# Sums of quarters one step earlier, and transfers given out in the opening

## The chip, the cores and the metric

The kernel runs on one core of a Trainium2 chip. The metric is the time of one execution in microseconds (us); the median of three runs is used, and 0.3% is about what a measurement of this kernel can tell from no change.

## The reference

Attention within chunks of 64 tokens, and behind it a gated feed-forward layer over all 4608 tokens, in float32:

```
q, k, v: (8, 8, 576, 64)              # batch, heads, tokens, width; 9 chunks of 64
scores = q_c @ k_c.T / 8              # within a chunk
attn   = softmax(scores)
x      = (attn @ v_c) laid out as (4608, 512)
g      = x @ w_gate                   # (512, 1536)
silu   = g / (1 + exp(-g))
val    = x @ w_val                    # (512, 1536)
out    = (silu * val) @ w_out         # (1536, 512)
```

## The kernel before

The tokens are cut into nine batches of 512 columns, and the inner width of 1536 into twelve pieces of 128. Handling one piece is a *step*, counted here from f = 0, so that the sixth step is step 5. A float32 number is held as two float32r parts, hi and lo, and a product of two such numbers is three matmuls (lo by hi, hi by lo, hi by hi), since `x` and the weights are split so everywhere.

The first two batches (`a0`, `a1`) go through the twelve steps together, while the weights come in for the first time. The weights arrive as raw 64-bit words; ScalarE (ACT) and VectorE (DVE) make float32 of them (`scale`, `shift`, `below`, `join`), split them (`upper` on ACT, `lower` on DVE), and what is made is stored to DRAM for the later batches (`save_w` the weights of gate and value, `save_o` those of the output).

A plain step does four products of 12 matmuls on TensorE (PE): gate and value of batch 0, gate and value of batch 1, and between them the projection of the step before (12 matmuls): 60 matmuls. In the steps from `SEVEN` on (`first_seven`) the four products of the two batches are made by Strassen's scheme instead: seven products of 6 matmuls, of sums of quarters of the weights with sums of quarters of x, 54 matmuls with the projection. For these are needed:

- four sums of the quarters of x, S1, S2, S4 and S5 (`Raw`, made by DVE: `whole` adds the hi and lo of a part of x, `both` combines two), and their hi and lo (`upper` on ACT, `lower` on DVE). Their places are the tiles w8 and w9; the split ones lie in w0 to w3, where the weights of steps 0 to 3 had been, once these are stored.
- in each step the sums of quarters of the next step's weights (`Quarters`: `sums` on DVE into `ts`, `upper` on ACT, `lower` on DVE). Their place, `th`, has one buffer in the steps up to `SEVEN`, and `save` stores it in two halves (`t<-th` in the profile). From `SEVEN` on every second step uses the place of batch 1's first x instead (`odd_t`).

The order of the work on PE, ACT and DVE is the order of the code, and in these first steps that of the transfers on the SyncE queue (SP) as well: each engine takes its instructions in that order, and one that waits holds up all behind it. In steps 1 to `SEVEN` - 1, `ahead`, `beside` and `within` are tables by step: what stands in them is put in before the gate's product, behind the shifts of the raw words, and behind the multiplication of batch 0's gate by its value. That multiplication (`times`, L519) reads the value's PSUM bank and so frees it for PE; there are two such banks (`ps_gv`) for the four products in turn.

Before step 1 stands an opening with a written order of its own (`opening`), in which the scores and columns of the two batches and step 0 are computed. Its loads are issued on SP in the first 15 us.

The later batches are computed from the stored weights; the change doesn't touch them.

Of the kernel before, what the change touches and what calls it, by code (L numbers as in the profile page):

```python
# [8 lines left out]
F32 = mybir.dt.float32  # L9
# [5 lines left out]
ALU = mybir.AluOpType  # L15
AX = mybir.AxisListType

P = 128
# [4 lines left out]
NK = DM // P  # L23
# [10 lines left out]
def attn_then_gated_ffn(ctx: ExitStack, tc: tile.TileContext, qk, v, wgv, wo, out):  # L34
# [102 lines left out]
    class Quarters:  # L137
# [12 lines left out]
            engine.tensor_tensor(out=s[:, 3], in0=t[:, 1], in1=s[:, 2], op=ALU.subtract)  # L150

        def place(self):
            if self.f >= SEVEN and self.f % 2:
                if not odd_t:
                    odd_t.extend(xs.tile([P, 4 * Q], F32R, name="th", tag=tag) for tag in ("xh0", "xl0"))
                return list(odd_t)
            both = const.tile([P, 2, 4 * Q], F32R, name="th", tag="th")
            return [both[:, 0], both[:, 1]]
# [11 lines left out]
                nc.sync.dma_start(out=kept_t[self.f][:, j], in_=self.halves[j].bitcast(F32))  # L170

    odd_t = []
    SEVEN, EARLY = 6, 4

    def moved(i):
        return f"w{(i + EARLY) % NF}"
# [18 lines left out]
    def save_w(f):  # L195
        kept_w[f] = store.tile([P, 2, 4 * Q], F32, name=f"w{f}")
        nc.sync.dma_start(out=kept_w[f], in_=w_both[f].bitcast(F32))
# [290 lines left out]
    def save_o(f):  # L488
        nc.sync.dma_start(out=kept_o[f], in_=out_now[f].bitcast(F32))
# [229 lines left out]
    for do in opening.split():  # L719
        if do[0] == ".":  # L720
            keep_warm(int(do[1:]))
        elif do[0] in "gvw":
            getattr(weights[do[:-1]], steps[do[-1]])()
        elif do[0] in "GV":
            if do[0] not in products:
                products[do[0]] = Product(a0, 0, "GV".index(do[0]))
            products[do[0]].add((int(do[3]), int(do[4])))
        elif do[0] == "e":
            a0.exchange(v0[int(do[1])][:, 1], values[int(do[1])][1], nc.scalar.copy)
        elif do == "H0":  # L730
            h0 = silu(products["G"].ps)
        elif do == "Q0":
            times(h0, products["V"].ps)
        else:
            b, i = int(do[1]), int(do[2])
            pairs = do[0] in "STCUL"
            getattr(couples[b, i // 2 if pairs else i], do[0])(i if pairs else int(do[3:] or 0))
    w = up[1]
    pg, pv = Product(a1, 0, 0), Product(a1, 0, 1)
    pg.add((0, 1), (1, 1), (0, 2), (1, 2), (2, 1), (3, 1), (2, 2), (3, 2))  # L740
# [5 lines left out]
    pv.add((0, 0), (1, 0), (2, 1), (3, 1), (2, 2), (3, 2), (2, 0), (3, 0))  # L746
    pv1 = pv.ps
    w.lower()
    o.shift()
    o.join()  # L750
    quarters = Quarters(1)
# [1 line left out]
    p0 = parts(a0, 0, h0)  # L753
    wo_f = out_weights(0)
    lag(p0, wo_f)
    down[1].load()
    down[1].scale()
    quarters.upper()

# [1 line left out]
    class Raw:  # L761


        def __init__(self):
            self.at = [const.tile([P, 2, NK // 2 * N], F32, name="sums", tag=tag) for tag in ("w8", "w9")]
            self.split = {}

        def place(self, i):
            return self.at[i[0]][:, i[1]]

        def whole(self, a, c, to):
# [22 lines left out]
    def begin():  # L794
        raw.append(Raw())
        raw[0].whole(a1, 0, S4)
        raw[0].whole(a1, 1, S1)

    ahead = {3: lambda: raw[0].upper(1, 0), 4: lambda: raw[0].upper(2, 1)}
    beside = {2: begin,  # L800
              3: lambda: (raw[0].whole(a0, 0, S2), raw[0].both(S4, S2, S4, ALU.subtract)),
              4: lambda: (raw[0].lower(2), raw[0].upper(4, 2)),
              5: lambda: (raw[0].whole(a0, 1, S5), raw[0].both(S5, S5, S2, ALU.subtract), raw[0].upper(5, 3))}
    within = {2: lambda: raw[0].both(S1, S1, S4, ALU.add),
              3: lambda: (raw[0].lower(1), raw[0].both(S2, S1, S2, ALU.subtract)),
              4: lambda: raw[0].lower(4), 5: lambda: raw[0].lower(5)}

    for f in range(1, SEVEN):
        w, o = up[f + 1], down[f]
        save_o(f - 1)  # L810
        up[f + 2].load()
        if f <= EARLY:
            save_w(f - 1)
        if f > 2:
            quarters.save()
        down[f + 1].load()
        ahead.get(f, lambda: None)()
        h0 = gate(a0, f)
        times(h1, pv1)
        put_off(h1)  # L820
        if f <= 2:
            quarters.lower()
            quarters.save()
        quarters = Quarters(f + 1)
        w.shift()
        w.below()
        pv0 = value(a0, f)
        o.shift()
        o.below()
        beside.get(f, lambda: None)()  # L830
        w.join()
        w.upper()
        times(h0, pv0)
        within.get(f, lambda: None)()
        p0 = parts(a0, f, h0)
        w.lower()
        o.join()
        quarters.sums(w.t)
        up[f + 2].scale()
        wo_f = out_weights(f)  # L840
        lag(p0, wo_f)
        h1 = gate(a1, f)
        quarters.upper()
        down[f + 1].scale()
        if f > 1:
            quarters.lower()
        pv1 = value(a1, f)
# [15 lines left out]
    def turns(which):  # L863

        if pending:
            project(*pending[0], which=which)
            if T - 1 in which:
                pending.pop()

    def first_seven(f, done, before):  # L870
# [29 lines left out]
        if w:  # L900
            w.join()
            w.upper()
        nc.scalar.copy(out=v2, in_=ps2)
        turns([0])
        product(ps1, 2, False)
        quarters = Quarters(f + 1)
        if w:
            quarters.sums(w.t)
            w.lower()
        nc.scalar.copy(out=v1, in_=ps1)  # L910
        if w:
            quarters.upper()
# [406 lines left out]
```

## Time and profile before

| | |
|---|---|
| runs, us | 902.27, 904.18, 905.06; median 904.18 |
| the profiled execution | 903.28, of which the span from first to last instruction is 901.5 |
| PE busy in the span | 885.2 (98%) |
| granted TensorE clock | 1.000 |
| mean of DMA moved | 248 GB/s |
| sizes of one transfer | weights stored `w<-w`, raw weights `raw<-in_wgv`, raw output weights `raw<-in_wo`: 1024 KB; `o<-both` and each half of `t<-th`: 512 KB; `h<-h`: 256 KB |
| silu of 128x512 on ACT | 599 ns (mean of L1153) |

A row of a timeline gives the start, the length, the engine (SPq and ACTq are the issues of transfers on SP and ACT), the line, the operation with output and input, and in brackets how long the engine stood idle ahead of it and what it waited for. A row of stretches gives the busy time of each engine between two moments, the granted clock, the share of time that the DMA engines were busy, and GB/s.

### The profile page before, as it was taken

To read this page: it belongs to the slowest core of one execution; us is meant where nothing else is said; L and a number is where in the kernel's file an instruction comes from. 1 tells how busy PE (TensorE), PEld (TensorE's weight loads), DVE (VectorE), ACT (ScalarE), POOL (GpSimd) and SP (SyncE) were. 2 spreads that over 40 slices of the span, in tenths; PEclk is the share of its full clock that TensorE was granted. 3 is DMA by queue.
4 is the path that set the end of the run, shared out by engine and by line. 5 is a ranking of instruction groups with operands and counts; after the bars stand their busy time and mean duration, and the time that the engine had idled before them with its cause. 6 is when DMAs were issued, how large, how long until landed. Compare 5 with 4: busy or idle time off the path is not lost.

```text
span 901.5 us, 14751 instructions
## 1 busy us (share of the span) xinstructions
PE 885.2 (98%) x6047; PEld 731.7 (81%) x6047; DVE 545.6 (61%) x834; ACT 386.1 (43%) x587; POOL 17.1 (2%) x18
## 2 busy tenths in 40 slices
PE   7998999999999999999999999999999999999998
PEld 6776788878888888888888888888888888888886
DVE  5869899853787655775763646776645533333332
ACT  4846677653514335324233445234334432223232
POOL 1200000000021000000000000000000000000000
PEclk9999999999999999999999999999999999999999
DMA  9297977799898657755586857665667565556651
GB/s 358 112 377 264 323 291 274 291 315 349 271 359 286 253 198 258 258 213 180 217 294 236 333 185 282 233 228 195 220 245 242 212 237 201 196 220 233 234 187 47
DMA packets 73170, 223.25 MB, mean 248 GB/s; under 512 B 30736, under 2 KB 30992, under 8 KB 58896
## 3 DMA queue, kind: packets, MB, share of 16 engines
q1 hardware_dynamic: 71664, 219.70, 67.3%
q10 hardware_dynamic: 1440, 2.62, 0.8%
q8 instruction: 47, 0.77, 0.3%
q14 instruction: 19, 0.16, 0.0%
HBM read 178.78 MB, written 43.52 MB: 247 GB/s over the span
## 4 chain that ended last, share of the span: by engine, by line
PE 90%; DMA 4%; DVE 4%; ACT 1%; issue 1%; POOL 0%; SPq 0%; ACTq 0%
PE ps_a L857 25%; PE ps_gv L857 19%; PE ps_o L538 11%; PE ps_o L539 10%; PE ps_o L540 10%; PE ps_gv L475 10%; DMA t<-th 3%; PE ps_a L287 2%; PE ps_a L365 1%; DMA qk_t<-in_qk 1%; ACT th L162 0%; DVE sums L776 0%; PE ps_a L451 0%; PE ps_a L465 0%; DVE th L165 0%
## 5 line engine op out<-in xcount | busy, mean ns | idle before, releaser
L857 PE MATMUL ps_a<-x,factors 128*128 128x512 f32 x864 | 219.3, 389 | 0.0
L857 PEld LDWEIGHTS ps_a<-x,factors 128*128 128x128 f32 x864 | 162.2, 188 | 33.7
L857 PE MATMUL ps_gv<-x,factors 128*128 128x512 f32 x648 | 164.5, 389 | 0.0
L857 PEld LDWEIGHTS ps_gv<-x,factors 128*128 128x128 f32 x648 | 121.7, 188 | 25.2
L538 PE MATMUL ps_o<-both,hl 128*128 128x512 f32 x336 | 132.3, 394 | 0.2 <-DVE hl L63 0.2
L539 PE MATMUL ps_o<-both,hh 128*128 128x512 f32 x336 | 131.0, 390 | 0.0
L540 PE MATMUL ps_o<-both,hh 128*128 128x512 f32 x336 | 130.9, 389 | 0.0
L475 PE MATMUL ps_gv<-xh,w 128*128 128x512 f32 x384 | 117.0, 390 | 0.2 <-ACT xh L614 0.2
L63 DVE TENSOR_TENSOR hl<-h,hh 128x512 fp32r<-128x512 f32 x98 | 67.6, 690 | 61.7 <-ACT hh L62 61.5
L62 ACT CAST hh<-h 128x512 fp32r<-128x512 f32 x98 | 60.4, 617 | 96.1 <-PE ps_o L540 51.3
L861 DVE TENSOR_TENSOR h<-h,ps_gv 128x512 f32<-128x512 f32 x42 | 28.8, 686 | 105.6 <-PE ps_gv L857 105.4
L352 DVE STREAM_TRANSPOSE turned<-s_sb 32x256 f32<-32x256 f32 x192 | 83.7, 436 | 2.7
L475 PEld LDWEIGHTS ps_gv<-xh,w 128*128 128x128 f32 x384 | 72.0, 188 | 15.7 <-issue 0.7
L519 DVE SCALAR_TENSOR_TENSOR h<-v,h 128x512 f32<-128x512 f32 x84 | 58.1, 692 | 37.7 <-ACT h L1153 33.0
L475 PE MATMUL ps_gv<-xl,w 128*128 128x512 f32 x192 | 74.0, 395 | 5.3 <-DVE h L519 2.9
L538 PEld LDWEIGHTS ps_o<-both,hl 128*128 128x128 f32 x336 | 63.1, 188 | 14.1 <-DVE hl L63 0.7
L540 PEld LDWEIGHTS ps_o<-both,hh 128*128 128x128 f32 x336 | 63.1, 188 | 13.2
L539 PEld LDWEIGHTS ps_o<-both,hh 128*128 128x128 f32 x336 | 63.1, 188 | 12.7
L1153 ACT ACTIVATE h<-ps_a 128x512 f32<-128x512 f32 x36 | 21.5, 599 | 112.2 <-PE ps_a L857 112.2
L861 DVE TENSOR_TENSOR v<-v,ps_a 128x512 f32<-128x512 f32 x42 | 28.8, 687 | 41.1 <-PE ps_a L857 36.4
L475 PEld LDWEIGHTS ps_gv<-xl,w 128*128 128x128 f32 x192 | 36.0, 188 | 14.2 <-DVE h L519 4.5
L1139 ACT ACTIVATE h<-h 128x512 f32<-128x512 f32 x36 | 22.8, 632 | 53.0 <-DVE h L861 52.9
(132 smaller groups left out, 1007.4 us busy)
## 6 DMA issues: line engine op xcount, KB each, us to landing
factors<-w SPq DMA_DIRECT2D x36, 1024.0 KB, 4.8
factors<-t SPq DMA_DIRECT2D x36, 1024.0 KB, 6.0
both<-o SPq DMA_DIRECT2D x70, 512.0 KB, 6.3
w<-w SPq DMA_DIRECT2D x16, 1024.0 KB, 9.7
t<-th SPq DMA_DIRECT2D x24, 512.0 KB, 5.8
two<-o SPq DMA_DIRECT2D x12, 1024.0 KB, 5.0
raw<-in_wgv SPq DMA_DIRECT2D x11, 1024.0 KB, 8.2
qk_t<-in_qk SPq DMA_DIRECT2D x10, 1024.0 KB, 8.4
```

Source lines behind the costliest of these rows:

```text
L62: nc.scalar.copy(out=hi, in_=src)
L63: (engine or nc.vector).tensor_tensor(out=lo, in0=src, in1=hi.bitcast(F32), op=ALU.subtract)
L352: nc.vector.transpose(out=self.turned[to:to + 32, p:p + 2, j, :, 32 * (i % 2):32 * (i % 2) + 32], in_=src[32 * i:32 * i + 32, :, o // 2, 3 ...
L475: nc.tensor.matmul(ps, w, x, start=first and (k, i) == which[0], stop=last and (k, i) == which[-1])
L519: nc.vector.scalar_tensor_tensor(out=h, in0=pv, scalar=2.0 ** -8, in1=h, op0=ALU.mult, op1=ALU.mult)
L538: nc.tensor.matmul(o, hl[:, ts], woh, start=f == a.steps[0], stop=False)
L539: nc.tensor.matmul(o, hh[:, ts], wol, start=False, stop=False)
L540: nc.tensor.matmul(o, hh[:, ts], woh, start=False, stop=f == a.steps[1])
L857: nc.tensor.matmul(ps, w[u][:, k], x[i][v][:, k], start=first and k == 0 and n == 0, stop=k == NK // 2 - 1 and n == 2, skip_group_check=True)
L861: nc.vector.tensor_tensor(out=t, in0=t, in1=ps, op=ALU.add)
L1139: nc.scalar.activation(h, h, AF.Silu, scale=2.0 ** -8)
L1153: nc.scalar.activation(h2, ps1, AF.Silu, scale=2.0 ** -8)
```

## The change

Four things are done.

1. `SEVEN` goes from 6 to 5: step 5 too is made by seven products.
2. The sums of x are made a step sooner: DVE makes S4 in step 1 (and the second of a0 for S5), S1 and the first of S2 in step 2, and so on; the last split (`upper(5, 3)`, `lower(5)`) now stands in step 5, the first by seven products. The tiles w8 and w9 are therefore taken one by one.
3. At the end of the opening's code `save_w(0)` and the loads of step 3's raw weights and of the second pair of raw output weights are issued, and `save_w(1)` behind the last subtraction for step 1's weights. Before, all of these stood in steps 1 and 2.
4. In steps 2 to 4 the load of raw weights stands ahead of `save_o`, and in steps 3 and 4 the store of the quarters ahead of `save_w`.

The diff:

```
@@ class Quarters
         def place(self):
-            if self.f >= SEVEN and self.f % 2:
+            if (self.f - SEVEN) % 2 and self.f > SEVEN:
...
-    SEVEN, EARLY = 6, 4
+    SEVEN, EARLY = 5, 4
@@ behind the loop over the opening
+    save_w(0)
+    up[3].load()
+    down[1].load()
+    down[2].load()
     w = up[1]
...
     w.lower()
+    save_w(1)
     o.shift()
...
     lag(p0, wo_f)
-    down[1].load()
     down[1].scale()
@@ class Raw
         def __init__(self):
-            self.at = [const.tile([P, 2, NK // 2 * N], F32, name="sums", tag=tag) for tag in ("w8", "w9")]
+            self.at = {}
             self.split = {}
 
         def place(self, i):
+            if i[0] not in self.at:
+                self.at[i[0]] = const.tile([P, 2, NK // 2 * N], F32, name="sums", tag=("w8", "w9")[i[0]])
             return self.at[i[0]][:, i[1]]
@@ the tables by step
     def begin():
         raw.append(Raw())
         raw[0].whole(a1, 0, S4)
-        raw[0].whole(a1, 1, S1)
-
-    ahead = {3: lambda: raw[0].upper(1, 0), 4: lambda: raw[0].upper(2, 1)}
-    beside = {2: begin,
-              3: lambda: (raw[0].whole(a0, 0, S2), raw[0].both(S4, S2, S4, ALU.subtract)),
-              4: lambda: (raw[0].lower(2), raw[0].upper(4, 2)),
-              5: lambda: (raw[0].whole(a0, 1, S5), raw[0].both(S5, S5, S2, ALU.subtract), raw[0].upper(5, 3))}
-    within = {2: lambda: raw[0].both(S1, S1, S4, ALU.add),
-              3: lambda: (raw[0].lower(1), raw[0].both(S2, S1, S2, ALU.subtract)),
-              4: lambda: raw[0].lower(4), 5: lambda: raw[0].lower(5)}
+
+    ahead = {3: lambda: raw[0].upper(1, 0), 4: lambda: (raw[0].upper(2, 1), raw[0].upper(4, 2))}
+    beside = {1: begin, 2: lambda: (raw[0].whole(a1, 1, S1), raw[0].both(S1, S1, S4, ALU.add)),
+              3: lambda: (raw[0].lower(1), raw[0].both(S4, S2, S4, ALU.subtract)),
+              4: lambda: (raw[0].lower(2), raw[0].both(S5, S5, S2, ALU.subtract))}
+    within = {1: lambda: raw[0].whole(a0, 1, S5), 2: lambda: raw[0].whole(a0, 0, S2),
+              3: lambda: raw[0].both(S2, S1, S2, ALU.subtract), 4: lambda: raw[0].lower(4)}
 
     for f in range(1, SEVEN):
         w, o = up[f + 1], down[f]
+        if f > 1:
+            up[f + 2].load()
         save_o(f - 1)
-        up[f + 2].load()
-        if f <= EARLY:
-            save_w(f - 1)
         if f > 2:
             quarters.save()
-        down[f + 1].load()
+            if f <= EARLY:
+                save_w(f - 1)
+        if f > 1:
+            down[f + 1].load()
         ahead.get(f, lambda: None)()
@@ first_seven
         nc.scalar.copy(out=v2, in_=ps2)
+        if f == SEVEN:
+            raw[0].upper(5, 3)
         turns([0])
...
             w.lower()
+        if f == SEVEN:
+            raw[0].lower(5)
         nc.scalar.copy(out=v1, in_=ps1)
```

What it makes of the order shows on SP at the end of the opening. Before, behind the last load of the opening (L236, the first raw output weights), up to the load of step 4's raw weights; o0 to t2 are places in DRAM, `w_116` and `w_659` the weights of steps 0 and 1:

```order
L236 DMA raw_136<-in_wo 128x2x512
L489 DMA o0_707<-both_704 128x1024
L109 DMA raw_714<-in_wgv 128x1024
L197 DMA w0_716<-w_116 128x2048
L236 DMA raw_718<-in_wo 128x2x512
L170 DMA t1_739<-th_711 128x1024 x2
L489 DMA o0_707<-both_775 128x1024
L109 DMA raw_828<-in_wgv 128x1024
```

The same stretch of SP now:

```order
L236 DMA raw_136<-in_wo 128x2x512
L197 DMA w0_661<-w_116 128x2048
L109 DMA raw_663<-in_wgv 128x1024
L236 DMA raw_665<-in_wo 128x2x512
L197 DMA w1_700<-w_659 128x2048
L489 DMA o0_715<-both_712 128x1024
L170 DMA t1_741<-th_719 128x1024 x2
L109 DMA raw_832<-in_wgv 128x1024
```

The store of the quarters, L170, had three transfers of 1024 KB between itself and `save_o` (L489) before; now it stands right behind `save_o`, and those three with a fourth (`w1`) stand ahead of both. The next raw load comes ahead of the next `save_o`.

On DVE, step 1 before, from the low half of the quarters (L165) on:

```order
L165 TENSOR_TENSOR th_711<-ts_696,th_711 128x1024
L83 TENSOR_SCALAR t_557<-t_557 128x1024
L83 TENSOR_SCALAR wo_708<-wo_708 128x512
L90 ISA t_557<-t_557 128x2048
L519 SCALAR_TENSOR_TENSOR h_733<-ps_gv_744,h_733 128x512
L63 TENSOR_TENSOR hl_764<-h_733,hh_763 128x512
L130 TENSOR_TENSOR w_760<-t_557,w_760 128x1024
```

The same now:

```order
L165 TENSOR_TENSOR th_719<-ts_704,th_719 128x1024
L83 TENSOR_SCALAR t_557<-t_557 128x1024
L83 TENSOR_SCALAR wo_716<-wo_716 128x512
L779 TENSOR_TENSOR sums_761<-xh0_102,xl0_103 128x1024
L90 ISA t_557<-t_557 128x2048
L519 SCALAR_TENSOR_TENSOR h_735<-ps_gv_746,h_735 128x512
L779 TENSOR_TENSOR sums_761<-xh1_108,xl1_109 128x1024
L63 TENSOR_TENSOR hl_769<-h_735,hh_768 128x512
L130 TENSOR_TENSOR w_764<-t_557,w_764 128x1024
```

Two sums of x (L779, which is L773 before) have come into step 1. And DVE in step 5, before, from the multiplication of step 4's last value on:

```order
L519 SCALAR_TENSOR_TENSOR h_1150<-ps_gv_1158,h_1150 128x512
L83 TENSOR_SCALAR t_1119<-t_1119 128x1024
L83 TENSOR_SCALAR wo_1154<-wo_1154 128x512
L773 TENSOR_TENSOR sums_871<-xh1_108,xl1_109 128x1024
L776 TENSOR_TENSOR sums_871<-sums_871,sums_870 128x1024
L90 ISA t_1119<-t_1119 128x2048
L519 SCALAR_TENSOR_TENSOR h_1192<-ps_gv_1199,h_1192 128x512
L786 TENSOR_TENSOR x_1216<-sums_871,x_1216 128x1024
```

The same step now, from the shift behind that multiplication to the addition into v (L866, which is L861 before):

```order
L83 TENSOR_SCALAR t_1121<-t_1121 128x1024
L90 ISA t_1121<-t_1121 128x2048
L148 TENSOR_TENSOR ts_1221<-t_1121 128x512
L149 TENSOR_TENSOR ts_1221<-t_1121,ts_1221 128x256
L150 TENSOR_TENSOR ts_1221<-t_1121,ts_1221 128x256
L130 TENSOR_TENSOR w_1207<-t_1121,w_1207 128x1024
L792 TENSOR_TENSOR x_1210<-sums_761,x_1210 128x1024
L83 TENSOR_SCALAR wo_1156<-wo_1156 128x512
L90 ISA wo_1156<-wo_1156,o_sb_1157 128x1024
L866 TENSOR_TENSOR h_1183<-h_1183,ps_gv_1182 128x512
L165 TENSOR_TENSOR th_1229<-ts_1221,th_1228 128x1024
L866 TENSOR_TENSOR v_1185<-v_1185,ps_a_1180 128x512
```

Of the three operations on x (L773, L776, L786) one is left, the last low half (L792), now between the weights' low half and the shift of the output weights; the other rows are those of any step by seven products.

## The prediction

> **What bounds the kernel now.** I read the page's busy table first, then the waits of the engines, then the busy time by stretch over the steps that the change touches, and last the rows around each wait. The busy table and the waits (engine, line, what it waited for: us in total, times, longest):
>
> ```profile
> PE 885.2 (98%) x6047; PEld 731.7 (81%) x6047; DVE 545.6 (61%) x834; ACT 386.1 (43%) x587; POOL 17.1 (2%) x18
> ...
> PE ps_gv L475 <- DVE h L519: 2.9, 4, 1.2
> ...
> PE ps_gv L475 <- ACT h L512: 1.7, 1, 1.7
> ```
>
> TensorE (PE) is the bound: only fewer matmuls, or fewer of its idle gaps, shorten the kernel. The gaps total 901.5 - 885.2 = 16.3 us, and five of them (2.9 + 1.7 us) are at L475, the plain products of steps 1 to 5. The step boundaries as first matmuls of a step on PE (start, length, idle before):
>
> ```profile
> 50.55 0.39 PE L475 MATMUL ps_gv<-xl,w 128*128 128x512 f32 x1
> 55.98 0.39 PE L475 MATMUL ps_gv<-xl,w 128*128 128x512 f32 x1
> 64.14 0.39 PE L475 MATMUL ps_gv<-xl,w 128*128 128x512 f32 x1
> 72.87 0.50 PE L475 MATMUL ps_gv<-xl,w 128*128 128x512 f32 x1 [1.66 <-ACT h L512]
> 90.31 0.50 PE L475 MATMUL ps_gv<-xl,w 128*128 128x512 f32 x1 [0.23 <-DVE h L519]
> 105.37 0.50 PE L475 MATMUL ps_gv<-xl,w 128*128 128x512 f32 x1 [1.17 <-DVE h L519]
> 116.39 0.39 PE L857 MATMUL ps_a<-xl,w 128*128 128x512 f32 x1
> ```
>
> From 50.55 (gate of batch 1, step 1) to 64.14 (the same of step 2) PE issues the 60 matmuls of one step without a gap: 13.59 us. Step 2 begins at 55.98, step 6 (the first by seven products) at 116.39. The four steps between would take 4 x 13.59 = 54.36 us and take 60.41: **6.05 us are lost**. By step (length, then PE, PEld, DVE, ACT, POOL busy, clock, DMA share, GB/s), steps 2, 3, 4, 5 and then 6, 7:
>
> ```profile
> 55.98:72.87 16.89, 14.06 (x62) 11.01 (x60) 11.53 (x15) 7.44 (x10) 0.00 (x0) 1.00 0.77 306
> 72.87:87.19 14.32, 14.03 (x61) 11.29 (x61) 13.66 (x18) 8.58 (x11) 0.00 (x0) 1.00 0.87 309
> 87.19:101.32 14.13, 13.90 (x61) 11.19 (x60) 12.07 (x17) 9.52 (x12) 0.00 (x0) 1.00 0.93 333
> 101.32:116.39 15.07, 13.90 (x61) 11.19 (x60) 12.39 (x16) 9.66 (x12) 0.00 (x0) 1.00 0.90 317
> 116.39:128.75 12.36, 12.36 (x55) 10.04 (x54) 11.59 (x16) 8.75 (x14) 0.00 (x0) 1.00 0.71 262
> 128.75:141.00 12.25, 12.25 (x56) 10.14 (x54) 11.05 (x16) 9.11 (x14) 0.00 (x0) 1.00 0.86 330
> ```
>
> The losses over 13.59 are 3.30, 0.73, 0.54 and 1.48 us. Where they come from stands on ACT and DVE:
>
> ```profile
> 60.88 1.05 ACT L162 CAST th<-ts 128x1024 fp32r<-128x1024 f32 x1 [6.47 <-DMA t<-th]
> ...
> 102.41 1.05 ACT L162 CAST th<-ts 128x1024 fp32r<-128x1024 f32 x1 [2.95 <-DMA t<-th]
> ...
> 61.97 1.23 DVE L165 TENSOR_TENSOR th<-ts,th 128x1024 fp32r<-128x1024 f32 x1 [5.02 <-ACT th L162]
> ...
> 103.49 1.23 DVE L165 TENSOR_TENSOR th<-ts,th 128x1024 fp32r<-128x1024 f32 x1 [3.51 <-ACT th L162]
> ```
>
> The tile th has one buffer. ACT may not write the next step's quarter sums into it before the store of the last ones (t<-th) has landed; DVE stands behind ACT, and behind that DVE instruction stands everything else DVE owes PE: the L519 product that frees a PSUM buffer. Why the store lands late is in the SyncE (SP) queue and in the DMA issues (size, us from issue to landing; first the store of step 1, then that of step 6):
>
> ```profile
> 44.33 0.34 SPq L489 DMA_DIRECT2D o<-both  x1
> 44.77 0.38 SPq L109 DMA_DIRECT2D raw<-in_wgv  x1
> 45.19 0.72 SPq L197 DMA_DIRECT2D w<-w  x1
> 46.01 0.43 SPq L236 DMA_DIRECT2D raw<-in_wo  x1
> 46.53 1.38 SPq L170 DMA_DIRECT2D t<-th  x2
> ...
> t<-th SPq DMA_DIRECT2D x2, 512.0 KB, 12.9
> ...
> 116.01 0.33 SPq L489 DMA_DIRECT2D o<-both  x1
> 116.54 1.58 SPq L170 DMA_DIRECT2D t<-th  x2
> ...
> t<-th SPq DMA_DIRECT2D x2, 512.0 KB, 3.6
> ```
>
> With 0.5 + 1 + 1 + 1 = 3.5 MB (sizes in the table above) issued in the 2.2 us ahead of it the store takes 12.9 us, with 0.5 MB ahead 3.6 us. And just before, the queues are empty (two stretches, columns as above; at the end the two rows that the opening's transfers wait for in the change: batch 1's columns on PE, and the low half of step 1's weights on DVE):
>
> ```profile
> 32.00:35.00 3.00, 3.00 (x53) 2.50 (x55) 0.92 (x2) 2.97 (x6) 0.00 (x0) 1.00 0.00 0
> ...
> 38.00:41.00 3.00, 3.00 (x14) 2.46 (x14) 2.86 (x6) 2.04 (x4) 0.00 (x0) 1.00 0.00 0
> ...
> 34.42 2.23 PE L465 MATMUL ps_a<-pT,v_t 64*64 64x64 f32 x128
> ...
> 39.18 1.22 DVE L130 TENSOR_TENSOR w<-t,w 128x1024 fp32r<-128x1024 f32 x1
> ```
>
> **The change part by part.** *Step 5 by seven products.* It issues 54 matmuls for 60. By the rows a step of the one kind takes 13.59 us and of the other 12.25 (step 7): -1.34 us, all on PE. Every projection stays.
>
> *The transfers given out in the opening.* The store of step 0's weights, the load of step 3's raw weights and that of the second pair of raw output weights, 3 MB, go out long before step 1's store; only save_o's 0.5 MB stays freshly ahead of it. The store of step 1's weights, 1 MB, now comes before it too and waits for the L130 row, to 40.4. The raw loads wait for the columns, to 36.7. At the 306 to 333 GB/s of the stretches above, the 3 MB that come after 36.7 take 10 us, to 47: what is left over when the store goes out at 46.5 (under 0.5 MB, 1.5 us) puts its landing 3.6 to 6 us after its issue, at 50 to 53 us instead of 60.8. ACT wants it about 55 (its cast there began its wait at 60.88 - 6.47 = 54.4, and DVE's work ahead of it grows by 2.3 us, below). The 5.02 us of DVE idleness go. What these transfers cost in the opening: nothing is queued behind them on SP until 44.33, and PE issues 56 matmuls in 12.25 us at share 0.86 as it does 14 in 3.00 at share 0.00 (0.22 and 0.21 us each); I take 0.
>
> In steps 2 to 4 the raw load now stands ahead of save_o, which waits for DVE, so it goes out up to a step early, and the store of the quarters stands ahead of the weight store. Each store of quarters has 0.5 MB freshly issued ahead of it, as in the row with 3.6 us; so has step 4's, the one that ends the wait of the 102.41 row. It is issued within 1.5 us of the step's start and wanted 11 to 12 us after it, so 8 us of reserve stand against it.
>
> *DVE's work.* Twelve operations of 128x1024 for the sums of x move. One costs its distance to the next on DVE:
>
> ```profile
> 81.10 1.22 DVE L786 TENSOR_TENSOR x<-sums,x 128x1024 fp32r<-128x1024 f32 x1
> 82.23 1.22 DVE L776 TENSOR_TENSOR sums<-sums 128x1024 f32<-128x1024 f32 x1
> ```
>
> that is 1.13 us. Steps 1 to 5 had 0, 3, 4, 2, 3 of them; now they have 2, 3, 3, 3, 1. Step 3, with 4, is 13.66 us of DVE; with 3 it is 12.5; step 2 stays at 11.5, and step 4, with one more, goes from 12.07 to 13.2: 37.3 us in the three for PE's 40.8. Step 1 has DVE idle anyway before 61.97. So no step of 60 matmuls is DVE's any more, and once DVE isn't held by the store it keeps up: its L519 product for the last value is due 2.7 us (12 matmuls) after the step's start, and comes within 1 us. The losses of 3.30, 0.73 and 0.54 us were one backlog, made by the 5.02 us and carried by step 3's 13.66: they go, -4.57. Step 5's 1.48 us come from the 3.51 us: -1.48.
>
> *The last low half in step 5.* One 1.13 us operation is put into a step of 12.25 us on PE with 11.1 us of DVE work. PE needs DVE there before the seventh product (it overwrites the bank that DVE adds into v):
>
> ```profile
> 125.83 0.68 DVE L861 TENSOR_TENSOR v<-v,ps_a 128x512 f32<-128x512 f32 x1
> ...
> 126.62 0.44 PE L857 MATMUL ps_a<-xl,th 128*128 128x512 f32 x1
> ```
>
> In step 6, which DVE entered late (behind the 103.49 row's backlog), this add ended at 126.51, 0.11 us before PE. One operation more would make PE wait up to 1.0 us; if DVE enters on time, none. DVE should enter within 0.2 us of time, so I take 0.2 and keep 0 to 1.0.
>
> *ACT's casts* (two of 1.05 us at the head of step 4, one in step 5): ACT is busy 9.5 of 14 us in step 4, and the gate's silu behind them isn't due for 2.7 us. 0, at most 0.3.
>
> The sum: -1.34 - 4.57 - 1.48 + 0.2 = **-7.2 us**. The profiled execution took 903.28 us, 0.90 under the median of 904.18: 896.1 for it, **897.0** for the median.
>
> **The rivals.**
>
> *1. Backlog stays.* DVE's work meets PE's within 1 us a step, and small gaps keep it behind: steps 3 and 4 lose their 0.73 + 0.54 again and step 5 pays 1.0. The 0.23 us row at 90.31 speaks for it, the 12.5 against 13.59 us against it. -7.39 + 1.27 + 1.0 = -5.1: 899.1. With it can come the store of h. ACT issues it in each step and, as the change's instructions wait in steps 1 and 2, the second silu of the step may not start before it has landed:
>
> ```profile
> 90.28 0.33 ACTq L577 DMA_DIRECT2D h<-h  x1
> ...
> h<-h ACTq DMA_DIRECT2D x1, 256.0 KB, 10.0
> ```
>
> Issued 3.1 us into step 4, landed at 13.1, plus 0.6 of silu (599 ns in the table above): 13.7 against a step of 13.59, so 0.1 us a step at that landing, and 1 us for each us later.
>
> The Trainium skill (DMA: Bandwidth & Descriptors, Queues, rings and completion order) has each DMA engine take turns between the queues packet by packet, so a store on ACT's queue wouldn't stand behind SP's megabytes; with the page's fixed 2.0 us (measured there for DMAs issued by GpSimd) and half of its 436 GB/s an estimate is 3.2 us. The 10.0 us of this trace speak against it, so I leave h in this rival; by the page it would drop out.
>
> *2. The store lands late all the same* in step 1: the 4 MB in the pause don't drain, because the raw load waits for the columns until 36.7 and the rest queues behind. If the store lands after 60, the first three losses stay, and -1.34 - 1.48 + 0.2 = -2.6 is left: 901.6, not told from no change. For it: 3 MB in the 10 us before it. Against it: at 306 GB/s, worked out above, it is still 2 us early at worst.
>
> *3. Slower.* A raw load stands ahead of save_o and the quarters' store in SP's queue, and waits itself for its buffer. If one in each of steps 2, 3 and 4 went out only 8 us into the step, the store behind it would miss its date as step 1's does now, and each step would lose 3.30: 9.9 for 4.57, less the 1.34 + 0 of step 5: +4.0, 908.2. It decides from 8 us on. Against it: the raw buffers were read out three steps earlier, so that the loads can go as soon as they are reached.
>
> **How the numbers follow.** Within 0.3% is 2.7 us here, about what can't be told from no change. Forecast (-6.3 to -7.6) 0.70; rival 1 (-3 to -6.3) 0.19; rival 2 0.07; rival 3 0.04. Faster: 0.70 + 0.19 less 0.01 for its end = 0.88; same 0.08; slower 0.04. The range: the low end is all 7.4 us and 1.9, by which the lowest run lies under the median, 895; the high end takes rival 1 with h at 1 us in two steps, -7.39 + 1.27 + 1.0 + 2.0 = -3.1, 901.0.
>
> **What would show it.** PE's waits at L475 on L519 and on L512 (4.5 us) are gone from the list after the first 50 us; steps 2, 3 and 4 take 13.6 us each, step 5 12.3 to 12.5; L857 has 42 matmuls more and L475 48 fewer. The cast L162 doesn't wait for t<-th, whose landing is under 8 us in each step, and the 32 to 41 us stretch moves over 200 GB/s. Step 6's first matmul comes at 109.0 to 109.4 for 116.39, and all later is the same, moved. Wrong it would be if a cast L162 still waits for t<-th, if PE waits before the seventh product of step 5 by more than 1 us, or if the waits behind 110 us grow.

## The result, and the profile after

The changed kernel takes 897.37 us (median of four runs, 896.41 to 897.63) against 903.98 us (902.27 to 905.06): a ratio of 0.9927, 95% interval 0.9909 to 0.9944. The forecast was 897.0 us, in a range of 895 to 901. A second set of five runs gave 896.85 us (ratio 0.9924, 0.9912 to 0.9937). Of all the runs in this document one, of the kernel with the sums a step sooner, took 1270.18 us at a granted clock of 0.655, and it is left out of that kernel's median.

The profiled execution took 897.35 us with a span of 895.2 us, 6.3 us less than before. In the changed kernel the line numbers behind line 770 are five or six higher: the seventh products stand at L862 (L857 before), the add into v at L866 (L861), the whole sums at L779 (L773), sums of two at L782 (L776), low halves at L792 (L786).

The busy table, the two groups of plain products at L475 (count, busy, mean ns, idle before them) and what is left of PE's waits there:

```profile
PE 883.8 (99%) x6041; PEld 731.2 (82%) x6041; DVE 548.2 (61%) x837; ACT 388.0 (43%) x590; POOL 17.0 (2%) x18
...
L475 PE MATMUL ps_gv<-xh,w 128*128 128x512 f32 x352 | 107.1, 390 | 0.1
...
L475 PE MATMUL ps_gv<-xl,w 128*128 128x512 f32 x176 | 67.5, 393 | 0.3 <-DVE h L519 0.3
...
PE ps_gv L475 <- DVE h L519: 0.3, 1, 0.3
```

L475 has 528 matmuls (576 before), and the four waits on DVE and the one on ACT, 4.6 us together, have become one of 0.3 us. The steps 2 to 6 now (length, then PE, PEld, DVE, ACT, POOL busy, clock, DMA share, GB/s):

```profile
55.97:69.57 13.60, 13.60 (x61) 11.11 (x60) 11.64 (x15) 6.45 (x9) 0.00 (x0) 1.00 0.63 213
69.57:83.88 14.31, 14.01 (x62) 11.27 (x61) 13.17 (x19) 9.69 (x13) 0.00 (x0) 1.00 0.90 348
83.88:97.48 13.60, 13.60 (x62) 11.27 (x60) 13.01 (x17) 10.28 (x14) 0.00 (x0) 1.00 0.81 305
97.48:110.06 12.58, 12.54 (x56) 10.06 (x54) 11.96 (x17) 8.91 (x13) 0.00 (x0) 1.00 0.84 324
110.06:122.30 12.24, 12.24 (x56) 10.13 (x54) 11.05 (x16) 9.11 (x14) 0.00 (x0) 1.00 0.68 245
```

Steps 2 and 4 lose nothing, step 3 still loses 0.71 us (14.31 for 13.60), and step 5, now of 54 matmuls, takes 12.58 where 12.24 would do. Step 6 begins at 110.06 instead of 116.39. Behind that nothing changed. From step 7's first matmul to the end of the span, first in the changed kernel and then in the kernel before (columns as above):

```profile
122.30:895.20 772.90, 768.48 (x5043) 635.81 (x5041) 444.61 (x683) 306.35 (x473) 7.89 (x5) 1.00 0.67 241
```

```profile
128.75:901.50 772.75, 768.13 (x5043) 635.89 (x5041) 443.82 (x683) 306.19 (x473) 7.90 (x5) 1.00 0.67 241
```

772.90 us and 772.75: the whole difference lies ahead of step 7. The larger part of it comes from the store of the quarters. SP's queue at the end of the opening, the landings of that store issued at 44.72, and ACT's cast that waited for it (6.47 us before):

```profile
24.82 0.34 SPq L197 DMA_DIRECT2D w<-w  x1
36.73 0.34 SPq L109 DMA_DIRECT2D raw<-in_wgv  x1
37.16 0.67 SPq L236 DMA_DIRECT2D raw<-in_wo  x1
40.40 0.33 SPq L197 DMA_DIRECT2D w<-w  x1
44.30 0.33 SPq L489 DMA_DIRECT2D o<-both  x1
44.72 1.63 SPq L170 DMA_DIRECT2D t<-th  x2
...
t<-th SPq DMA_DIRECT2D x2, 512.0 KB, 7.5
...
54.88 1.05 ACT L162 CAST th<-ts 128x1024 fp32r<-128x1024 f32 x1 [0.39 <-ACT h L512]
```

The raw load and the output weights go out at 36.7 and 37.2, the weight store at 40.4, as the forecast had read from the rows of before. The two halves of the quarters, issued at 44.72 and 46.03, land 7.6 and 7.3 us later, at 52.4 and 53.4. The cast at 54.88 is the same one as that of 60.88 before, and it waits for ACT's own work only.

What still stops PE in step 3 stands in four places, in order of time: ACT's cast of the low words (L87) in step 2, DVE's whole sum behind it, the L519 product of step 3 and PE's matmul.

```profile
58.95 0.60 ACT L512 ACTIVATE h<-ps_gv 128x512 f32<-128x512 f32 x1 [2.46 <-PE ps_gv L475]
...
59.45 1.11 ACT L87 ACTIVATE t<-raw 128x1024 int32<-128x1024 uint32 x1
...
60.59 1.23 DVE L779 TENSOR_TENSOR sums<-xh,xl 128x1024 f32<-128x1024 f32 x1 [1.60 <-ACT t L87]
...
72.11 0.68 DVE L519 SCALAR_TENSOR_TENSOR h<-ps_gv,h 128x512 f32<-128x512 f32 x1
...
72.16 0.39 PE L475 MATMUL ps_gv<-xh,w 128*128 128x512 f32 x1
72.84 0.50 PE L475 MATMUL ps_gv<-xl,w 128*128 128x512 f32 x1 [0.30 <-DVE h L519]
73.18 0.63 PE L475 MATMUL ps_gv<-xh,w 128*128 128x512 f32 x2
```

The tile of the sum S1 lies in the place `w8`, which holds step 3's raw words (`if f == 3: return "w8"` in `Up.at`). DVE may write S1 only when ACT has read the low half of these words, and ACT does that behind the gate's silu (L512), which itself waits 2.46 us for PE. DVE stands idle for 1.60 us, and is then so far behind that the L519 product of step 2's last value, which stands in step 3, frees its bank too late and PE waits 0.30 us. PE pays more than the 0.30: from 72.16 to 72.84 is 0.68 us where two matmuls lie 0.23 apart, and the first one behind the gap takes 0.34 to the next, 0.11 more; 0.56 of the 0.71 us lie here.

In step 5 the place is the one that the forecast named, ahead of the seventh product. DVE's addition into v, which frees the bank for it, ends at 107.83:

```profile
107.15 0.68 DVE L866 TENSOR_TENSOR v<-v,ps_a 128x512 f32<-128x512 f32 x1
...
107.45 0.39 PE L540 MATMUL ps_o<-both,hh 128*128 128x512 f32 x1
107.88 0.50 PE L862 MATMUL ps_a<-xl,th 128*128 128x512 f32 x1
108.22 0.63 PE L862 MATMUL ps_a<-xh,th 128*128 128x512 f32 x2
```

From 107.45 to 107.88 are 0.43 us where 0.23 is usual, and then 0.34 for 0.23: together 0.31 of the 0.34 us that step 5 takes over 12.24.

### The profile page after: what moved, and what is told of

It is laid out like the page before. It is cut to its first block, busy times and chain, and to the rows that moved or that the text cites. A ratio compares the mean times of both kernels' runs of the same rounds, so it can differ in the third digit from the quotient of the medians.

```text
span 895.2 us, 14746 instructions
## 1 busy us (share of the span) xinstructions
PE 883.8 (99%) x6041; PEld 731.2 (82%) x6041; DVE 548.2 (61%) x837; ACT 388.0 (43%) x590; POOL 17.0 (2%) x18
## 4 chain that ended last, share of the span: by engine, by line
PE 92%; DVE 3%; DMA 2%; issue 1%; ACT 1%; POOL 0%; SPq 0%; DVEq 0%; ACTq 0%; POOLq 0%
PE ps_a L862 26%; PE ps_gv L862 20%; PE ps_gv L475 11%; PE ps_o L538 11%; PE ps_o L540 10%; PE ps_o L539 10%; DMA v_t<-in_v 2%; PE ps_a L287 2%; DVE turned L352 1%; PE ps_a L365 1%; DMA qk_t<-in_qk 0%; DVE h L519 0%; PE ps_a L465 0%; DVE hl L63 0%; POOL v_t L408 0%
## 5 line engine op out<-in xcount | busy, mean ns | idle before, releaser
L862 PE MATMUL ps_a<-x,factors 128*128 128x512 f32 x864 | 219.2, 389 | 0.0
L862 PEld LDWEIGHTS ps_a<-x,factors 128*128 128x128 f32 x864 | 162.2, 188 | 33.7
L862 PE MATMUL ps_gv<-x,factors 128*128 128x512 f32 x648 | 164.4, 389 | 0.0
L862 PEld LDWEIGHTS ps_gv<-x,factors 128*128 128x128 f32 x648 | 121.7, 188 | 25.2
L538 PE MATMUL ps_o<-both,hl 128*128 128x512 f32 x336 | 132.2, 394 | 0.2 <-DVE hl L63 0.2
L475 PE MATMUL ps_gv<-xh,w 128*128 128x512 f32 x352 | 107.1, 390 | 0.1
L866 DVE TENSOR_TENSOR h<-h,ps_gv 128x512 f32<-128x512 f32 x43 | 29.5, 686 | 106.1 <-PE ps_gv L862 105.9
L519 DVE SCALAR_TENSOR_TENSOR h<-v,h 128x512 f32<-128x512 f32 x86 | 59.5, 692 | 38.0 <-ACT h L1162 33.3
L475 PEld LDWEIGHTS ps_gv<-xh,w 128*128 128x128 f32 x352 | 66.0, 188 | 13.8 <-ACT xh L614 0.3
L538 PEld LDWEIGHTS ps_o<-both,hl 128*128 128x128 f32 x336 | 63.0, 188 | 14.1 <-DVE hl L63 0.7
L475 PE MATMUL ps_gv<-xl,w 128*128 128x512 f32 x176 | 67.5, 393 | 0.3 <-DVE h L519 0.3
L866 DVE TENSOR_TENSOR v<-v,ps_a 128x512 f32<-128x512 f32 x43 | 29.5, 687 | 40.7 <-PE ps_a L862 36.0
L866 DVE TENSOR_TENSOR v<-v,ps_gv 128x512 f32<-128x512 f32 x43 | 29.6, 687 | 24.3 <-PE ps_gv L862 24.2
```

Source lines behind the costliest of these rows:

```text
L475: nc.tensor.matmul(ps, w, x, start=first and (k, i) == which[0], stop=last and (k, i) == which[-1])
L519: nc.vector.scalar_tensor_tensor(out=h, in0=pv, scalar=2.0 ** -8, in1=h, op0=ALU.mult, op1=ALU.mult)
L538: nc.tensor.matmul(o, hl[:, ts], woh, start=f == a.steps[0], stop=False)
L862: nc.tensor.matmul(ps, w[u][:, k], x[i][v][:, k], start=first and k == 0 and n == 0, stop=k == NK // 2 - 1 and n == 2, skip_group_check=True)
L866: nc.vector.tensor_tensor(out=t, in0=t, in1=ps, op=ALU.add)
```

## The experiments

The opening itself ends at slightly different times from one profile to the next: step 1's first projection (L538) came between 47.32 and 48.17 us. So beside the times I use the distance D on PE from that matmul to the first one of step 6. It was 116.39 - 47.83 = 68.56 us before and 110.06 - 47.81 = 62.25 us after. The theory: the transfers take the loss of steps 2 to 5 away, and seven products in step 5 bring the rest. The rival: the sums of x, moved off step 3, do part of it, or something else late takes the transfers' gain.

**The transfers alone.** The kernel before, with only the new order of transfers:

```diff
+    save_w(0)
+    up[3].load()
+    down[1].load()
+    down[2].load()
     w = up[1]
...
     w.lower()
+    save_w(1)
     o.shift()
...
-    down[1].load()
     down[1].scale()
...
+        if f > 1:
+            up[f + 2].load()
         save_o(f - 1)
-        up[f + 2].load()
-        if f <= EARLY:
-            save_w(f - 1)
         if f > 2:
             quarters.save()
-        down[f + 1].load()
+            if f <= EARLY:
+                save_w(f - 1)
+        if f > 1:
+            down[f + 1].load()
```

> Step 5 stays a plain step and the sums of x stand where they stood before; only the transfers are given out as in the change (in the opening, and the order on SP in steps 1 to 5). Theory (the late store of the quarters held ACT and DVE): that store lands by 53 us, steps 2 and 5 lose nothing (3.30 and 1.48 us gone), and of the 0.73 and 0.54 us of steps 3 and 4 about half stays, since step 3 still has four sums: gain 5.0 to 5.5 us, about 898.7. Rival (the earlier sums carry the gain, the transfers little): gain under 2.5 us, 901.5 or more.

Measured: 897.49 us (897.05 to 897.92), ratio 0.9931 (0.9916 to 0.9945); D is 110.36 - 47.76 = 62.60 us. Steps 2 to 5, all of 60 matmuls:

```profile
55.92:69.52 13.60, 13.60 (x61) 11.27 (x60) 12.38 (x16) 6.91 (x10) 0.00 (x0) 1.00 0.54 193
69.52:83.16 13.64, 13.64 (x62) 11.29 (x61) 13.38 (x17) 7.94 (x12) 0.00 (x0) 1.00 0.96 363
83.16:96.76 13.60, 13.60 (x62) 11.16 (x60) 12.38 (x17) 10.55 (x14) 0.00 (x0) 1.00 0.81 311
96.76:110.36 13.60, 13.60 (x62) 11.26 (x60) 12.61 (x17) 8.79 (x12) 0.00 (x0) 1.00 0.74 291
```

All that was lost is gone, 5.96 us of D, where half of the losses of steps 3 and 4 had been expected to stay. Step 3 here still has the four operations on x of the kernel before, 13.38 us of DVE in 13.64 of PE, and loses nothing. So for DVE's sake nothing had to leave step 3; once the store lands in time, the four fit. The time is that of the whole change to 0.1 us, though step 5 has six matmuls more; by D the whole change is 0.35 us better.

**The rest alone.** The changed kernel with the old order of transfers (the lines above the other way round):

```diff
-    save_w(0)
-    up[3].load()
-    down[1].load()
-    down[2].load()
...
-        if f > 1:
-            up[f + 2].load()
         save_o(f - 1)
+        up[f + 2].load()
+        if f <= EARLY:
+            save_w(f - 1)
         if f > 2:
             quarters.save()
...
+        down[f + 1].load()
```

> Step 5 by seven products and the sums of x a step sooner, but every transfer where it stood before. Theory: the store of step 1 lands at about 61 us again, DVE stands idle 5 us ahead of the quarters' low half, step 2 loses about 3.3 us; steps 3 and 4 lose less than before; the store of step 4 lands late too, and now the first step by seven products waits for it, 1.5 us or more. Gain 0.5 to 2.5 us, 901.5 to 903.5. Rival (the earlier sums and the seven products carry the gain): 4 us or more, 900 or less.

Measured: 902.67 us (ten runs, 902.15 to 905.49), ratio 0.9991 (0.9981 to 1.0001): no difference that can be told. D is 68.02 us. (The profiled run was the slowest of the ten. From step 7's first matmul on it took 775.4 us for the 772.8 of before; that lies outside D.) The store holds ACT and ACT holds DVE as in the kernel before:

```profile
60.99 1.05 ACT L162 CAST th<-ts 128x1024 fp32r<-128x1024 f32 x1 [6.64 <-DMA t<-th]
...
62.08 1.22 DVE L165 TENSOR_TENSOR th<-ts,th 128x1024 fp32r<-128x1024 f32 x1 [5.26 <-ACT th L162]
```

Of the 1.34 us of the seven products 0.54 us of D is left, 0.88 by the medians; the same waits take the rest.

DVE comes to S1 two microseconds behind that, at 64.17, without a wait:

```profile
64.17 1.23 DVE L775 TENSOR_TENSOR sums<-xh,xl 128x1024 f32<-128x1024 f32 x1
```

**Half of the transfers each.** The kernel before with the new order inside steps 2 to 5 only, and then with the opening's transfers only. The core of the first:

```diff
+        if f > 1:
+            up[f + 2].load()
         save_o(f - 1)
-        up[f + 2].load()
-        if f <= EARLY:
+        if f == 1:
+            up[f + 2].load()
+        if f <= 2:
             save_w(f - 1)
         if f > 2:
             quarters.save()
+            if f <= EARLY:
+                save_w(f - 1)
         down[f + 1].load()
```

> The kernel before, with nothing but the order on SP in steps 2 to 5 as in the change (raw load ahead of save_o, quarters' store ahead of the weight store); the opening's transfers stay in step 1. Theory (two stores, two losses): step 1's store lands at 61 us as before and steps 2 to 4 lose their 3.30, 0.73 and 0.54 us, but step 4's store lands within 8 us and step 5's 1.48 us go: about 902.4, 1.0 to 1.5 us of gain. Rival (the order carries as much as the opening's transfers, for each store has less ahead of it): 3 us or more, 900.5 or less.

Measured: 901.80 us (ten runs, 901.23 to 903.42), ratio 0.9978 (0.9969 to 0.9988), D 66.76 us: 1.80 less than before, a little over the 1.0 to 1.5 expected. Step 5 loses nothing; steps 2 to 4 still do, the cast of step 1 waiting 6.27 us for the store:

```profile
60.00 1.05 ACT L162 CAST th<-ts 128x1024 fp32r<-128x1024 f32 x1 [6.27 <-DMA t<-th]
```

The core of the second:

```diff
+    save_w(0)
+    up[3].load()
+    down[1].load()
+    down[2].load()
     w = up[1]
...
         save_o(f - 1)
-        up[f + 2].load()
-        if f <= EARLY:
+        if f > 1:
+            up[f + 2].load()
+        if 2 < f <= EARLY:
             save_w(f - 1)
         if f > 2:
             quarters.save()
-        down[f + 1].load()
+        if f > 1:
+            down[f + 1].load()
```

> The kernel before, with the four transfers given out in the opening, but in steps 2 to 5 the old order on SP (save_o, raw load, weight store, quarters' store). Theory: step 1's store lands by 53 us and the 3.30, 0.73 and 0.54 us go; step 4's store, behind 2.5 MB, takes 10 to 12 us again and step 5 loses 1 to 1.5 us: 899 to 899.5, 4 to 4.5 us of gain. Rival (step 5's loss was backlog from step 2 too, and not its own store's): all 6 us, 897.5.

Measured: 899.70 us (898.87 to 900.57), ratio 0.9957 (0.9942 to 0.9971), D 63.26 us: 5.30 less than before. Steps 2 to 4 are free, and step 5 loses 0.68 us, less than the 1 to 1.5 expected, since step 4's store is still behind the others:

```profile
97.21 1.05 ACT L162 CAST th<-ts 128x1024 fp32r<-128x1024 f32 x1 [2.17 <-DMA t<-th]
...
98.30 1.23 DVE L165 TENSOR_TENSOR th<-ts,th 128x1024 fp32r<-128x1024 f32 x1 [2.79 <-ACT th L162]
```

So there are two late stores, each mended by its own part of the change: the one of step 1 (worth the more) by the opening, the one of step 4 by the order in the steps. The two gains come to 5.30 + 1.80 = 7.10 where both edits together bring 5.96. Of the 1.14 that is counted twice 0.80 is step 5's loss: 1.48 before, 0.68 with the opening alone and nothing with the order alone. Most of the rest is step 2's, which with the order alone took 16.47 us for 16.89.

**The sums a step sooner, without seven products in step 5.**

```diff
-    SEVEN, EARLY = 5, 4
+    SEVEN, EARLY = 6, 4
```

> The change with step 5 still a plain step of 60 matmuls: the transfers and the sums a step sooner are there, the seven products begin in step 6 as before. Theory (the sums' new places cost the 0.72 us of step 3 by DVE's wait for L87, and the seven products of step 5 gain 1.34 less 0.33): step 3 takes 14.3 us, all others 13.6, time 0.7 us over the kernel with the transfers alone, 898.2, and 0.9 over the change. Rival (the seven products gain nothing by themselves): like the change, 897.4, with the first matmul of step 6 at 110.1.

Measured: 898.52 us (three runs, 897.96 to 898.58), ratio 0.9941 (0.9921 to 0.9960), D 63.27 us. Against the transfers alone that is 0.67 us of D more. The same two rows as in the changed kernel stand there:

```profile
60.40 1.23 DVE L779 TENSOR_TENSOR sums<-xh,xl 128x1024 f32<-128x1024 f32 x1 [1.60 <-ACT t L87]
...
72.66 0.50 PE L475 MATMUL ps_gv<-xl,w 128*128 128x512 f32 x1 [0.30 <-DVE h L519]
```

Moving the sums is what costs step 3 its 0.7 us, whatever step 5 does. Seven products in step 5 then bring 63.27 - 62.25 = 1.02 us.

**The low words read sooner.** If the wait for `w8` is the cause, ACT reading the low words ahead of the gate's silu must end it. The changed kernel with

```diff
         ahead.get(f, lambda: None)()
+        w.below()
         h0 = gate(a0, f)
...
         w.shift()
-        w.below()
         pv0 = value(a0, f)
```

> The change, with one ACT operation of each plain step (the low word of the next raw weights, L87) put ahead of the silu of batch 0's gate instead of behind it. Theory (the 0.72 us that step 3 loses in the changed kernel come from DVE, which stands idle 1.60 us in step 2 until ACT has read the raw words out of w8, the place of the sum S1): DVE's wait for L87 falls under 0.3 us, PE's 0.30 us wait at 72.8 goes, step 3 takes 13.6 us, gain on the changed kernel 0.6 to 0.7 us, about 896.7. Rival (three sums in each of steps 2 and 3 are simply too much for DVE): step 3 still takes 14.2 us or more, no gain.

Measured: 895.98 us (895.30 to 896.81), ratio 0.9914 (0.9899 to 0.9929); D is 61.40 us. Steps 2 to 4 take 13.60 us each and step 5 12.44: of the 0.85 us by D 0.71 are step 3's and 0.14 step 5's. ACT's cast runs at 56 us, and DVE's S1 starts behind DVE's own work, two us sooner, without a wait:

```profile
55.99 1.13 ACT L87 ACTIVATE t<-raw 128x1024 int32<-128x1024 uint32 x1
...
58.50 1.22 DVE L779 TENSOR_TENSOR sums<-xh,xl 128x1024 f32<-128x1024 f32 x1
...
70.01 0.68 DVE L519 SCALAR_TENSOR_TENSOR h<-ps_gv,h 128x512 f32<-128x512 f32 x1
```

**DVE's idle time filled.** I had read the loss as the 1.60 us for which DVE stands idle. So I gave DVE work for that time: the sum S5 from step 1, put ahead of S1 in step 2.

```diff
-    beside = {1: begin, 2: lambda: (raw[0].whole(a1, 1, S1), ...),
+    beside = {1: begin, 2: lambda: (raw[0].whole(a0, 1, S5), raw[0].whole(a1, 1, S1), ...),
...
-    within = {1: lambda: raw[0].whole(a0, 1, S5), 2: lambda: raw[0].whole(a0, 0, S2),
+    within = {2: lambda: raw[0].whole(a0, 0, S2),
```

> The change, with the sum for S5 (1.13 us on DVE, place w9) moved from step 1 to step 2, ahead of S1, so that DVE has something to do while ACT reads the raw words out of w8. Step 2 then has four sums and step 3 three. Theory (step 3's 0.72 us come from DVE's idle 1.60 us): the wait for L87 shrinks to about 0.5 us and step 3 loses under 0.3 us: 0.4 to 0.7 us below the change. Rival (DVE's load is the limit): one sum more in step 2 makes steps 2 and 3 lose 1 us or more.

Measured: 897.06 us (896.35 to 897.60), ratio 0.9928 (0.9913 to 0.9943). Step 3 takes 14.32 us, as in the changed kernel:

```profile
60.38 1.23 DVE L779 TENSOR_TENSOR sums<-xh,xl 128x1024 f32<-128x1024 f32 x1 [0.49 <-ACT t L87]
...
72.64 0.50 PE L475 MATMUL ps_gv<-xl,w 128*128 128x512 f32 x1 [0.31 <-DVE h L519]
```

DVE's idle time went from 1.60 to 0.49 us as expected, but step 3 didn't feel it; the rival's 1 us or more isn't there either. S1 starts 11.5 us ahead of the L519 product of step 3 in both kernels (60.38 and 71.90 here, 60.59 and 72.11 in the changed kernel): its start is a date that ACT sets, and what counts is how much work stands between the two. The transfers alone show the other side: there S1 starts at the same date with only two sums of 1.13 us up to the L519 product instead of three, and the product runs at 70.82, 1.3 us sooner:

```profile
60.56 1.23 DVE L777 TENSOR_TENSOR sums<-xh,xl 128x1024 f32<-128x1024 f32 x1 [0.49 <-ACT t L87]
...
70.82 0.69 DVE L519 SCALAR_TENSOR_TENSOR h<-ps_gv,h 128x512 f32<-128x512 f32 x1
```

**Step 5's gap.** Two ways to take work of DVE from ahead of the seventh product. First, the output weights' shift and join behind the add into v, in the changed kernel:

```diff
-        o.shift()
-        o.join()
+        if f > SEVEN:
+            o.shift()
+            o.join()
...
         add(v2, ps1)
+        if f == SEVEN:
+            o.shift()
+            o.join()
```

> The change, with the two operations on the output weights in step 5 (shift and join, 0.9 us on DVE) put behind the addition into v that frees the bank for the seventh product. Theory (that addition, late by the low half moved into step 5, costs the 0.33 us that step 5 takes over 12.25): PE's gap ahead of the seventh product goes, step 5 takes 12.25 to 12.3 us, gain on the changed kernel 0.3 us, about 897.1. Rival (DVE's load in that step is the limit, whatever the order): the gap moves to step 6, no gain.

Measured: 897.01 us (896.86 to 897.78), ratio 0.9927 (0.9912 to 0.9942). Step 5 takes 12.24 us, its gap is gone; step 6 loses 0.95 us in its place, as the rival had it, because ACT waits for the joined weights and comes late with the copy that PE needs in step 6:

```profile
107.44 0.62 ACT L62 CAST both<-wo 128x512 fp32r<-128x512 f32 x1 [2.16 <-DVE wo L90]
...
113.39 0.98 PE L862 MATMUL ps_a<-x,th 128*128 128x512 f32 x3 [0.55 <-ACT h L901]
```

To step 7's first matmul the distance is 122.48 - 47.40 = 75.08 us, against 122.30 - 47.81 = 74.49 of the changed kernel: 0.59 us worse by the traces, which the times don't show.

Second, with the low words read sooner, the last low half of the quarters (`quarters.lower()`, L165), for which nobody waits that early:

```diff
         add(h, ps3)
-        if w:
+        if w and f > SEVEN:
             quarters.lower()
...
         add(v2, ps1)
+        if f == SEVEN:
+            quarters.lower()
```

> The kernel with L87 ahead of the gate's silu, and in step 5 the low half of the next quarters (L165, 1.13 us on DVE, not wanted before the second product of step 6) put behind the addition into v that frees the seventh product's bank. Theory: step 5 takes 12.25 us for 12.43, and step 6 takes no more than 12.25: 0.2 us below the kernel with L87 alone, about 895.8. Rival (as with the output weights: the gap only moves to step 6): 0 or a loss of up to 0.5 us.

Measured: 894.94 us (894.84 to 896.00), ratio 0.9906 (0.9892 to 0.9921), D 61.20 us. Steps 3 to 6:

```profile
69.93:83.53 13.60, 13.60 (x62) 11.27 (x60) 12.90 (x17) 9.09 (x13) 0.00 (x0) 1.00 0.99 385
83.53:97.13 13.60, 13.60 (x62) 11.26 (x60) 12.39 (x17) 9.56 (x13) 0.00 (x0) 1.00 0.79 295
97.13:109.37 12.24, 12.24 (x56) 10.13 (x54) 11.82 (x17) 8.58 (x13) 0.00 (x0) 1.00 0.83 316
109.37:121.65 12.28, 12.28 (x56) 10.09 (x54) 11.05 (x16) 9.16 (x14) 0.00 (x0) 1.00 0.69 245
```

No step loses anything. This is the version that beats both kernels. Since its distance to the changed kernel is small, both ran once more, on one chip, with the kernel before:

> The changed kernel once more, on the same chip as the kernel with L87 ahead and the quarters' low half later: 897 to 898 us.

> The kernel with L87 ahead of the gate's silu and the quarters' low half later in step 5, beside the changed kernel on one chip. Theory: 0.72 + 0.33 us less than the change, 896.2 to 896.7 if the change takes 897.3. Rival (chips differ, the kernels don't): within 0.5 us of the change.

Measured: 896.85 us (895.97 to 897.79) for the change and 895.15 us (894.95 to 895.77; ratio to the kernel before 0.9906, 0.9893 to 0.9920) for the version. D came out at 109.59 - 47.32 = 62.27 and 61.20 us, within 0.02 us of the first time. The version is 1.07 us better by D, 1.70 us by the medians, whose runs don't overlap.

## Why the prediction was right, and where it was not

The gain of D, by the runs that take one part at a time (transfers alone; then the sums; then step 5):

| part | D, us | its share, us | predicted, us |
|---|---|---|---|
| before | 68.56 | | |
| transfers | 62.60 | -5.96 | -4.57 - 1.48 = -6.05 |
| sums of x a step sooner | 63.27 | +0.67 | 0 |
| seven products in step 5 | 62.25 | -1.02 | -1.34 + 0.2 = -1.14 |
| all | | -6.31 | -7.2 |

Taken up to step 7's first matmul instead of step 6's, the three shares are -6.10, +0.85 and -1.19 us: where step 6 is the first by seven products, it has the last low half of x in it and takes 12.40 us for 12.24.

The median of 897.37 lies nearer to the forecast of 897.0 than the sum deserves, for by D the sum is 0.9 us too large. For the profiled execution it had given 896.1, which took 897.35; that the medians agree to 0.4 us is in part the chance of single runs.

*The transfers.* Right in the mechanism, and in size to 0.1 us: the two experiments that leave one half of them out show the cast L162 waiting for t<-th again, each at its own store. Rival 2 (the store lands late all the same) and rival 3 (the raw load holds the stores) are excluded by the landings: 7.5 us in step 1, and in the next steps 4.7, 3.3, 3.8 and 3.9 us, for 8 us allowed.

*How the opening drains.* The working of this term was less good than its result. The store was to land 3.6 to 6 us after its issue and took 7.5, and the stretch from 32 to 41 us was to move over 200 GB/s and moved 123:

```profile
32.00:41.00 9.00, 8.87 (x163) 7.51 (x162) 6.07 (x10) 7.80 (x14) 0.00 (x0) 1.00 0.34 123
```

Only one of the transfers (24.82) goes out ahead of 36.7, and it landed 8.2 us later, at 33.0; the rest goes out at 36.7 to 40.4, so that about two of its 3 MB move behind 41 (9 us at 123 GB/s are 1.1 MB). The forecast's own dates left this stretch empty for its first half, and the mark didn't follow from them. That the 3 MB would drain by 47 was nearly right: the last store landed 7.5 us behind 40.4, at 47.9. The term held, but by a small reserve: the second half of the store lands at 53.4, and ACT is free for its cast at 54.5. In the second profile of the changed kernel it lands at 53.9 for a cast at 54.39, and with the transfers alone at 54.3 for a cast at 54.37.

*DVE keeps up.* This is the step that failed: "once DVE isn't held by the store it keeps up: its L519 product for the last value is due 2.7 us (12 matmuls) after the step's start, and comes within 1 us." In step 3 it comes at 72.11, 2.54 us behind the step's start, and ends at 72.79, when PE's next matmul had been due at 72.39. The working had added up DVE's busy time by step and never asked what each sum waits for. S1 is written into the place that holds step 3's raw words, and ACT reads these behind the gate's silu. S1 stood in step 2 before the change too: the list of the change, by which the sums come a step sooner, doesn't hold for S1. But before, S4 stood right ahead of it, and the store's stall held DVE so long that the two ran at 64.05 without a wait:

```profile
64.05 2.36 DVE L773 TENSOR_TENSOR sums<-xh,xl 128x1024 f32<-128x1024 f32 x2
```

The change moved S4 from ahead of S1 into step 1, and the first sum for S2 from step 3 to behind S1. Step 2 has three sums as before, and 11.64 us of DVE for 11.53, but three of them now run from S1 on, behind ACT's date, instead of two. With the old transfers this doesn't show, for the store holds DVE until 62.08, and S1 runs at 64.17 without a wait. With that stall gone ACT's date is what is late next. Rival 1 (a backlog because DVE's work meets PE's within 1 us a step) named the symptom and gave 1.27 us for steps 3 and 4; its other half, the silu held by the store of h, wasn't seen. The loss is not a rate: the transfers alone put 13.38 us of DVE into step 3 and lose nothing, and the changed kernel puts 13.17 there and loses 0.71.

*Step 5.* Seven products are worth 13.60 - 12.24 = 1.36 us, and 0.34 us were paid, nearly all ahead of the seventh product, for 0.2 taken; step 5 took 12.58 us where the forecast's mark was 12.3 to 12.5. In the version with both later edits, the low half of the quarters behind the add, they are gone. Which of DVE's operations ahead of the add is to blame isn't shown: the gap ended when the output weights' two were moved behind it, and also, with the low words read sooner, when the quarters' low half was. The sum is -1.02 for -1.14.

*The rest.* ACT's casts cost nothing, at 10.28 us of ACT in step 4. Nothing behind step 7 changed (0.15 us in 773). L475 has 48 matmuls fewer and L862 42 more, six fewer in sum: 6041 for 6047 in the busy table. The first matmul of step 6 came at 110.06, 0.7 us past the mark of 109.0 to 109.4, by step 3's loss.

## What to carry to other kernels

A stall that is taken away uncovers the dates behind it. Look up for each operation that stood behind the stall which tile it writes, who still reads that tile and behind what this reader stands. An operation that is put in behind such a date can cost time even where another one leaves from ahead of it and the step's sum stays the same. Busy sums by step (by the forecast 12.5 us of work in 13.6) don't show that; the date from which a chain of work may start and the work up to where it is wanted do. And a late store is best looked for in what was issued to its queue in the microseconds ahead of it: the same store landed 12.9 us after its issue with 3.5 MB given out in the 2.2 us ahead of it, 7.5 us with 0.5 MB just ahead and 3 MB in the 8 us before, and 3.3 to 4.7 us with 0.5 MB.

## What the runs showed of the hardware

A wait that the profile gives as 0.30 us cost PE 0.56: the start of the matmul behind it was 0.45 us late, and the one after that started 0.34 us later instead of 0.23. In step 5 a gap to which the profile names no releaser cost 0.31 in the same two parts. In both places PE paid 0.11 us beyond the late start itself.

The store of h, 256 KB on ACT's own queue, took as long as transfers of four times its size on SP's queue beside it. Here is step 5's stretch in the changed kernel; in step 4 of the kernel before it took 10.0 us.

```profile
raw<-in_wo SPq DMA_DIRECT2D x1, 1024.0 KB, 6.7
raw<-in_wgv SPq DMA_DIRECT2D x1, 1024.0 KB, 8.7
...
h<-h ACTq DMA_DIRECT2D x1, 256.0 KB, 8.0
```

In step 5 of the kernel with the transfers alone SP gave out nothing between 97.5 and 101.9 us, and the store of h, issued at 99.68, landed in 2.0 us.

The Trainium skill (DMA: Bandwidth & Descriptors, Queues, rings and completion order) has each DMA engine take turns between queues packet by packet, from which, with that page's fixed 2.0 us and half of its 436 GB/s, a landing of 3.2 us was estimated. The trace's 8.0 us is 2.5 times that estimate; which part of the estimate fails here isn't shown. No engine waited for that store, so it cost nothing.
